# Raw weight tiles moved ahead of all matmul operands, so that weights, x and activations start at one remainder modulo 512 bytes

## The chip, the core and the metric

The kernel runs on one core of a Trainium2 chip. Times are device microseconds (us) of one execution. The kernel before takes 596.16 us (median of 3 runs, 596.13 to 596.34). The execution that was profiled took 596.7 us, and its span from the first to the last instruction is 594.9 us.

A core has TensorE (PE in the profile; its weight loads are listed apart as PEld), VectorE (DVE), ScalarE (ACT), GpSimd (POOL), SyncE (SP, which issues most transfers here) and 16 DMA engines. SBUF is the on-chip memory: 128 partitions, and a tile takes the same stretch of bytes in each of them. PSUM holds the sums that TensorE writes.

## The reference

```
attention (2 batches, 8 heads, 768 positions, 64 wide): a window of 32 positions
    plus one summary key and value per block of 32, softmax  -> x (1536 x 512)
layer 0:  h = x @ w_in;   g = max(0.01 h, h);              x = g @ w_out
layer 1:  h = x @ w_in2;  g = h * tanh(softplus(h));       out = g @ w_out2
w_in 512 x 2048, w_out 2048 x 512; tokens 1536; float32
```

## The kernel before

Attention comes first, interleaved with the first products of layer 0 by an order written out by hand. From about 150 us on there are only the two layers.

**Slots.** The hidden width of 2048 is cut into 16 columns of 128 (f). The 1536 tokens are cut into three blocks j of 512. A slot is one f for one block: "up" (L504) makes h for it, 12 matmuls of 128x128 weights with 512 moving columns; ACT and DVE (and POOL in layer 1) turn h into g; "down" (L559 in layer 0, L566 in layer 1) adds g times the output weights to four sums y, 12 matmuls again. The 12 are four pieces by three products: every operand is held as a high and a low part (float32r), and high*high, high*low and low*high are added. Down lags up by three slots (`LAG = 3`), so TensorE runs up of slot n, down of slot n-3, up of slot n+1, and so on, in groups of 12. L580 is the down step of the last two slots. In up and in down of layer 0 the weights are the operand that is loaded and x or g moves; in down of layer 1, g is loaded and the weights move.

**Parts.** `PARTS = [(0, 6), (0, 10), (1, 10), (1, 6)]`: layer 0 takes its 16 f as 6 and 10, layer 1 as 10 and 6, and each part goes over the three blocks. So the parts have 6, 10, 10 and 6 slots per block.

**Weights.** Each slot's pair of weight tiles has a place k, and a part gives its slots these k, in order: part 0 has 0 to 5; parts 1 and 2 have 6 to 9 and then 0 to 5; part 3 has 6 to 9, 0, 1. A weight block comes by DMA into a `raw` tile (3 buffers, 4104 bytes in a partition, L147), is taken apart by ACT (L158), DVE (L165) and ACT (L194), and its low part is made by POOL or DVE (L201).

**Where tiles stand.** Pools are laid out in the order in which they are opened, each buffer rounded up to 32 bytes, and the pool decides where a tile is:

```
pool = wsp if k < PARTS[0][1] else post
w = pool.tile([P, 2, DM], F32R, tag=f"w{io}_{k}", name="w")
```

`wsp` (places 0 to 5), `xp` (x), `bigp`, `midp`, `l1p` and `gp` (g) follow `const`; then come `rawp` and `padp`. The attention's pools stand behind these, and when the attention is done (`att.close()`), `post` takes the same stretch for the weight places 6 to 9, the temporaries u and r of layer 1 and one more `mid` buffer. Within a weight, x or g tile every operand starts at a multiple of 512 bytes from the tile's start. In the built program of before, `wsp` begins at byte 17280 of a partition, which is 384 modulo 512, and the sizes of all pools up to g are multiples of 512: weights of places 0 to 5 (bytes 21376 on), x (70528 to 119680) and g (148352 on) have remainder 384. The three raw tiles take 4128 bytes each and `two` takes 32, so the attention's pools and later `post` begin at byte 177152, remainder 0.

So 4 of the 10 slots per block in parts 1 and 2, and 4 of the 6 in part 3, use weights at remainder 0 against x and g at 384: 36 slots, 864 matmuls. All other slots have both operands at 384.

Of the kernel before, what the change touches and what calls it, by code (L numbers as in the profile page):

```python
# [9 lines left out]
F32 = mybir.dt.float32  # L10
# [18 lines left out]
def kernel(  # L29
# [18 lines left out]
    P = 128  # L48
# [9 lines left out]
    NS = S // SB  # L58
# [36 lines left out]
    rscale = math.sqrt(D)  # L95

    const = ctx.enter_context(tc.tile_pool(name="const", bufs=1))
    wsp = ctx.enter_context(tc.tile_pool(name="wsp", bufs=1))
    xp = ctx.enter_context(tc.tile_pool(name="xp", bufs=1))
    bigp = ctx.enter_context(tc.tile_pool(name="bigp", bufs=1))  # L100
    midp = ctx.enter_context(tc.tile_pool(name="midp", bufs=4))
    l1p = ctx.enter_context(tc.tile_pool(name="l1p", bufs=2))
    gp = ctx.enter_context(tc.tile_pool(name="gp", bufs=LAG + 1))
    rawp = ctx.enter_context(tc.tile_pool(name="rawp", bufs=3))
    padp = ctx.enter_context(tc.tile_pool(name="padp", bufs=1))
    ps = ctx.enter_context(tc.tile_pool(name="ps", bufs=1, space=PSUM))

    ident = const.tile([P, P], F32, name="ident")
    ind = const.tile([P, 64], F32, name="ind")
    two = padp.tile([P, 1], F32, name="two")  # L110

    nc.scalar.preload_act_table_set("natural_log_exp_and_others")

# [500 lines left out]
    if True:  # L614
# [112 lines left out]
        with tc.manual_schedule(engines={ET.PE, ET.Activation, ET.DVE, ET.Pool}):  # L727
            for word in ORDER.split():
                name, _, banks = word.partition(":")
                eng = engines.get(name[-1])  # L730
                name = name.rstrip("adp") if eng else name
# [100 lines left out]
```

## Time and profile before

| | |
|---|---|
| median of 3 runs | 596.16 us |
| profiled execution | 596.7 us |
| its span | 594.9 us |
| PE busy | 586.1 us, 99% |
| DVE, ACT, POOL busy | 65%, 53%, 33% |

The page gives the busy time of each engine, the granted clock of TensorE, the chain of work that ended last (followed back from the last instruction), and groups of like instructions. Busy time of PE counts a matmul from its start to its modelled end, so consecutive matmuls overlap and a mean of 393 ns says nothing of the pace. The pace is read from the chain: a row "2.72 PE h L504 x12" is 12 matmuls that took 2.72 us of the chain, one after another.

### The profile page before, as it was taken

To read this page: it belongs to the slowest core of one execution; us is meant where nothing else is said; L and a number is where in the kernel's file an instruction comes from. 1 tells how busy PE (TensorE), PEld (TensorE's weight loads), DVE (VectorE), ACT (ScalarE), POOL (GpSimd) and SP (SyncE) were. 2 spreads that over 40 slices of the span, in tenths; PEclk is the share of its full clock that TensorE was granted. 3 is DMA by queue.
4 is the path that set the end of the run, shared out by engine and by line. 5 is a ranking of instruction groups with operands and counts; after the bars stand their busy time and mean duration, and the time that the engine had idled before them with its cause. 6 is when DMAs were issued, how large, how long until landed. Compare 5 with 4: busy or idle time off the path is not lost.

```text
span 594.9 us, 9052 instructions
## 1 busy us (share of the span) xinstructions
PE 586.1 (99%) x3302; PEld 476.0 (80%) x3302; DVE 384.7 (65%) x777; ACT 313.6 (53%) x671; POOL 194.5 (33%) x214
## 2 busy tenths in 40 slices
PE   9799999999999999999999999999999999999997
PEld 4688877787888888888888878888888888888885
DVE  6799865366541123115454998887699988777784
ACT  5878965467741223125655645554476555445442
POOL 6866841184410001003520323232232233232221
PEclk9999999999999999999999999999999999999999
DMA  9996454047631000002536210000022000010011
GB/s 321 331 345 214 161 170 138 2 135 246 221 106 37 0 2 0 1 0 81 171 121 227 74 35 1 0 1 0 1 71 73 0 1 0 2 39 33 0 72 71
DMA packets 19373, 52.10 MB, mean 88 GB/s; under 512 B 2176, under 2 KB 5248, under 8 KB 19072
## 3 DMA queue, kind: packets, MB, share of 16 engines
q1 hardware_dynamic: 18752, 51.00, 26.0%
q8 instruction: 26, 0.43, 0.3%
q10 hardware_dynamic: 576, 0.52, 0.3%
q14 instruction: 19, 0.16, 0.1%
HBM read 48.37 MB, written 3.15 MB: 87 GB/s over the span
## 4 chain that ended last, share of the span: by engine, by line
PE 90%; DMA 5%; ACT 2%; DVE 1%; POOL 0%; issue 0%; SPq 0%; DVEq 0%; ACTq 0%
PE h L504 42%; PE y L566 21%; PE y L559 21%; DMA raw<-in_moe_w_in_dram 3%; PE a L470 2%; PE a L406 2%; PE a L451 1%; DMA v<-in_v_dram 1%; PE y L580 1%; ACT top L158 1%; DMA kT<-in_kT_dram 1%; DVE mid L165 1%; ACT s L430 1%; ACT w L194 0%; ACT g L516 0%; POOL w L201 0%
## 5 line engine op out<-in xcount | busy, mean ns | idle before, releaser
L504 PE MATMUL h<-x,w 128*128 128x512 f32 (+1 forms) x1188 | 287.5, 388 | 0.2 <-ACT g L516 0.2
L504 PEld LDWEIGHTS h<-x,w 128*128 128x128 f32 x1188 | 218.2, 188 | 47.8 <-ACT g L516 0.6
L559 PE MATMUL y<-g,w 128*128 128x512 f32 (+1 forms) x612 | 143.5, 381 | 0.0
L566 PE MATMUL y<-w,g 128*128 128x512 f32 x552 | 136.4, 393 | 0.0
L222 POOL TENSOR_TENSOR g<-e,g 128x512 fp32r<-128x512 f32 x47 | 72.7, 1548 | 185.9 <-ACT g L219 178.3
L559 PEld LDWEIGHTS y<-g,w 128*128 128x128 f32 x612 | 110.1, 189 | 22.4
L566 PEld LDWEIGHTS y<-w,g 128*128 128x128 f32 x552 | 103.5, 188 | 23.8 <-ACT g L219 0.3
L201 POOL TENSOR_TENSOR w<-mid,w 128x512 fp32r<-128x512 f32 x45 | 63.2, 1412 | 106.4 <-ACT w L194 94.8
L520 DVE TENSOR_TENSOR g<-t,g 128x512 fp32r<-128x512 f32 (+1 forms) x51 | 37.2, 731 | 87.5 <-ACT g L516 87.4
L515 ACT ACTIVATE t<-h 128x512 f32<-128x512 f32 (+1 forms) x51 | 28.8, 565 | 90.5 <-PE h L504 90.5
L165 DVE SCALAR_TENSOR_TENSOR mid<-raw,top 128x512 int32<-128x512 int32 x64 | 56.4, 890 | 29.7 <-POOL w L201 17.2
L158 ACT ACTIVATE top<-raw 128x512 f16<-128x512 bf16 x64 | 50.2, 796 | 26.0 <-DMA raw<-in_moe_w_in_dram 10.3
L531 ACT ACTIVATE e<-h 128x512 f32<-128x512 f32 x48 | 28.6, 596 | 61.5 <-PE h L504 54.0
L542 DVE SCALAR_TENSOR_TENSOR u<-u,r 128x512 f32<-128x512 f32 x48 | 36.9, 769 | 25.5 <-ACT r L535 25.1
L534 ACT ACTIVATE r<-u,two 128x512 f32<-128x512 f32 x48 | 34.8, 724 | 30.0 <-DVE u L533 30.0
L430 ACT ACTIVATE s<-s,nm 128x120 f32<-128x120 f32 x96 | 36.6, 385 | 16.7 <-DVE nm L420 16.6
L194 ACT CAST w<-mid 128x512 fp32r<-128x512 f32 x61 | 37.0, 616 | 11.5 <-DVE mid L165 5.9
L219 ACT CAST g<-e 128x512 fp32r<-128x512 f32 x48 | 29.6, 616 | 25.4 <-DVE e L544 25.4
L533 DVE SCALAR_TENSOR_TENSOR u<-e 128x512 f32<-128x512 f32 x48 | 34.6, 721 | 1.1
L445 POOL TENSOR_TENSOR s<-s,r 128x480 f32<-128x480 f32 x24 | 25.0, 1043 | 27.8 <-DVE r L440 15.2
L543 DVE SCALAR_TENSOR_TENSOR u<-u,r 128x512 f32<-128x512 f32 x48 | 33.1, 691 | 1.4
L544 DVE SCALAR_TENSOR_TENSOR e<-e,u 128x512 f32<-128x512 f32 x48 | 33.1, 689 | 1.1
(72 smaller groups left out, 433.3 us busy)
## 6 DMA issues: line engine op xcount, KB each, us to landing
raw<-in_moe_w_in_dram SPq DMA_DIRECT2D x32, 512.0 KB, 3.9
raw<-in_moe_w_out_dram SPq DMA_DIRECT2D x32, 512.0 KB, 3.7
vw<-in_vW_dram SPq DMA_DIRECT2D x24, 192.0 KB, 5.1
kT<-in_kT_dram SPq DMA_DIRECT2D x8, 400.0 KB, 6.6
out_dram<-yp SPq DMA_DIRECT2D x12, 256.0 KB, 2.0
q<-in_qT_dram SPq DMA_DIRECT2D x20, 128.0 KB, 5.2
vS<-in_vS_dram SPq DMA_DIRECT2D x2, 1024.0 KB, 6.8
v<-in_v_dram SPq DMA_DIRECT2D x2, 768.0 KB, 8.9
```

Source lines behind the costliest of these rows:

```text
L158: (tc.keep_in_program_order if pin else id)(nc.scalar.mul(out=do, in_=di, mul=4.0))
L165: nc.vector.scalar_tensor_tensor(out=d, in0=wraw.pop(i)[:, 0:2 * DM].rearrange("p (f w) -> p f w", w=2)[:, :, 1], scalar=13, in1=wtop.pop( ...
L194: nc.scalar.copy(out=w[:, 0], in_=wmid[i])
L201: (eng or nc.gpsimd).tensor_sub(out=w[:, 1], in0=wmid.pop(i), in1=w[:, 0].bitcast(F32))
L222: (nc.vector if lo == "dve" else nc.gpsimd).tensor_sub(out=dst_lo, in0=src, in1=dst_hi.bitcast(F32))
L430: nc.scalar.activation(out=s[:, n], in_=s[:, n], func=AF.Exp, scale=-1.0, bias=nm[:, n:n + 1], accum_out=sm[:, n:n + 1],)
L504: nc.tensor.matmul(ph[:, 0:n], w[:, a, kt * P:(kt + 1) * P], x[:, c, kt, o:o + n], start=(kt == 0 and i == 0), stop=(kt == KT - 1 and i == 2),
L520: (eng or nc.vector).tensor_sub(out=g[:, 1, 0:n], in0=t[:, 0:n], in1=g[:, 0, 0:n].bitcast(F32))
L534: nc.scalar.activation(out=r, in_=u, func=AF.Ln, bias=two[:, 0:1])
L542: V.scalar_tensor_tensor(out=u, in0=u, scalar=2.0, in1=r, op0=ALU.add, op1=ALU.mult)
L559: mm = nc.tensor.matmul(y[d][:, o:o + n], w[:, a, d * P:(d + 1) * P], g[:, c, 0:n], start=sta and not second, stop=sto,)
L566: nc.tensor.matmul(y[d], g[:, a, d * P:(d + 1) * P], w[:, c], start=sta, stop=sto,)
```

## The change

`rawp` is opened directly behind `const`, ahead of `wsp`. The pool `padp` is gone, its tile `two` is in `const`, and `ind` has 44 columns instead of 64 (no slice of it reaches further than column 44).

```
-    wsp = ...   xp ... gp ... rawp ... padp        (order of before)
+    rawp = ctx.enter_context(tc.tile_pool(name="rawp", bufs=3))     (ahead of wsp)
-    rawp = ctx.enter_context(tc.tile_pool(name="rawp", bufs=3))
-    padp = ctx.enter_context(tc.tile_pool(name="padp", bufs=1))
-    ind = const.tile([P, 64], F32, name="ind")
-    two = padp.tile([P, 1], F32, name="two")
+    ind = const.tile([P, 2 * NS - 4], F32, name="ind")
+    two = const.tile([P, 1], F32, name="two")
```

In the built program the instructions of every engine stand in the same order with the same shapes; only addresses differ (and the width of the one memset of `ind`):

| tiles | before: byte, remainder modulo 512 | after |
|---|---|---|
| raw (3) | 164736, 168864, 172992: 384, 416, 448 | 17248, 21376, 25504: 352, 384, 416 |
| weights of places 0 to 5 | 21376 on: 384 | 33728 on: 448 |
| x0, x1, x2 | 86912, 103296, 70528: 384 | 99264, 115648, 82880: 448 |
| g (4) | 148352 on: 384 | 160704 on: 448 |
| attention's q, vw, pT; later weights of places 6 to 9 | 177152 on: 0 | 177088 on: 448 |
| ident | 16512: 128 | 16512: 128 |

## Rows read from the trace of the kernel before

**Rows 1.** Page, part 1: engine, busy us (share of the span), instructions.

```profile
PE 586.1 (99%) x3302; PEld 476.0 (80%) x3302; DVE 384.7 (65%) x777; ACT 313.6 (53%) x671; POOL 194.5 (33%) x214
```

**Rows 2.** Page, part 2: granted TensorE clock in 40 slices, tenths of full.

```profile
PEclk9999999999999999999999999999999999999999
```

**Rows 3.** Page, part 4: the chain that ended last, by engine.

```profile
PE 90%; DMA 5%; ACT 2%; DVE 1%; POOL 0%; issue 0%; SPq 0%; DVEq 0%; ACTq 0%
```

**Rows 4.** Waits of PE, 130 to 595 us: us in total, times, longest.

```profile
PE h L504 <- ACT g L516: 0.2, 1, 0.2
```

**Rows 5.** Chain, 240 to 270 us (part 1): start us, us, what.

```profile
240.06 2.76 PE h L504 x12
242.81 2.79 PE y L559 x12
245.61 2.75 PE h L504 x12
248.36 2.72 PE y L559 x12
...
256.52 2.72 PE h L504 x12
...
261.97 2.79 PE h L504 x12
264.76 2.76 PE y L559 x12
```

**Rows 6.** Chain, 395 to 426 us (part 2, layer 1).

```profile
408.75 2.79 PE y L566 x12
411.54 2.73 PE h L504 x12
414.27 2.72 PE y L566 x12
```

**Rows 7.** Lines of PE, 154.24 to 585.90 us: count | busy us, mean ns | idle.

```profile
L504 PE MATMUL h<-x,w 128*128 128x512 f32 x924 | 227.7, 393 | 0.0
L566 PE MATMUL y<-w,g 128*128 128x512 f32 x552 | 136.4, 393 | 0.0
L559 PE MATMUL y<-g,w 128*128 128x512 f32 x396 | 97.0, 393 | 0.0
```

**Rows 8.** Chain of the whole span: start us, us, what.

```profile
137.50 3.21 DMA raw<-in_moe_w_in_dram
142.56 3.04 PE h L504 x12
...
154.24 2.77 PE y L559 x12
...
348.26 2.89 PE y L566 x12
353.43 2.88 PE y L566 x12
...
585.90 5.47 PE y L580 x24
```

**Rows 9.** Two stretches: us, busy PE, PEld, DVE, ACT, POOL; clock, DMA share, GB/s.

```profile
0.00:50.00 50.00, 44.93 (x574) 35.38 (x574) 41.71 (x166) 38.20 (x136) 36.39 (x81) 1.00 0.99 329
430.00:480.00 50.00, 50.00 (x219) 40.85 (x219) 46.85 (x73) 32.36 (x54) 13.25 (x9) 1.00 0.14 43
```

**Rows 10.** Line L158: duration in ns min/median/max of its 64 instructions.

```profile
L158 ACT ACTIVATE top<-raw x64: 768/796/815, 10.5 to 456.3; 128x512 f16<-128x512 bf16 x64
```

**Rows 11.** Page, part 6: transfers, count, KB each, median us to landing.

```profile
raw<-in_moe_w_in_dram SPq DMA_DIRECT2D x32, 512.0 KB, 3.9
raw<-in_moe_w_out_dram SPq DMA_DIRECT2D x32, 512.0 KB, 3.7
vw<-in_vW_dram SPq DMA_DIRECT2D x24, 192.0 KB, 5.1
q<-in_qT_dram SPq DMA_DIRECT2D x20, 128.0 KB, 5.2
```

More of the change, by code (lines that the diff above doesn't have):

```diff
@@ L97 @@
     const = ctx.enter_context(tc.tile_pool(name="const", bufs=1))
+    rawp = ctx.enter_context(tc.tile_pool(name="rawp", bufs=3))
     wsp = ctx.enter_context(tc.tile_pool(name="wsp", bufs=1))
```

## The prediction

> **What bounds the kernel now.** I read the page first. PE is busy 99% of the span [rows 1], its clock was granted in full in all 40 slices [rows 2], and PE holds 90% of the chain that ended last, DMA 5% [rows 3]. The waits of PE say whether anything else sets its pace behind the attention: from 130 us on they find one wait of 0.2 us [rows 4]. So from about 150 us on the time is the number of matmuls times their pace, and only a change of the pace moves the end.
>
> The pace is in the chain. In part 1, groups of 12 matmuls of the same shape do not take the same time [rows 5]. Up and down groups alternate there, down three slots behind, so each row has its slot. The group at 242.81 is down of the block's fourth slot, whose weights have place 9, remainder 0 against 384 of g: 2.79 us. From 248.36 to 256.52 all operands have remainder 384: 2.72 us each. At 261.97 the next block begins, with place 6 again: 2.79 us. The groups at 245.61 and 264.76 have equal remainders but come right behind a slow group: 2.75 and 2.76 us. Layer 1 shows the same with the operands exchanged, where g is loaded and the weights move: 2.79 us at 408.75, 2.73 behind it, then 2.72 [rows 6]. So there are three paces: 2.72 us (226.7 ns a matmul) where remainders agree, 2.79 to 2.80 (232.5 to 233 ns) where they differ, and something between right behind a slow group.
>
> **The change, part by part.** No instruction is added, removed or moved on any engine or queue; the sum is one of paces.
>
> Weights of places 6 to 9: the 864 matmuls of the 36 slots that use them are 72 groups. At 0.07 to 0.075 us each that is 5.0 to 5.4 us. Equal groups right behind a slow one: in a block of 10 slots the order up, down of three slots earlier gives 7 of them (three downs between the first four ups, then the ups and the down that follow the four slow downs), in a block of 6 slots 4. That is 6 x 7 + 3 x 4 = 54; at 0.01 to 0.04 us (2.73 to 2.76 against 2.72) 0.5 to 2.2 us. Together 5.5 to 7.6 us if every group comes to 2.72.
>
> The whole stretch gives the same sum without a count by hand. From the group at 154.24 to the start of L580 at 585.90 [rows 8] are 431.66 us and 924 + 552 + 396 = 1872 matmuls [rows 7], 156 groups. At 2.72 us they would take 424.3 us: 7.3 us less. Two groups hold a delay that the remainders do not explain, 2.89 and 2.88 us against 2.80 [rows 8]; I leave them their 0.17 us. That makes 7.2 us, the value I take; it is at the upper end of the count by hand, which rounds the groups to 0.01 us.
>
> Ahead of 154 us the weights of places 0 to 5 already agree with x and g, and one slow group falls in front of 142.56, where PE follows a transfer of raw weights (137.50) and the group took 3.04 us [rows 8]. What PE gains ahead of that it waits away: 0. At the end L580 has equal remainders, 5.47 us for two groups, at most 0.03 us more: 0.
>
> The weight transfers of part 2 start when places are freed by PE, so they come earlier with it. The tightest engine behind PE is DVE: 46.85 of 50 us from 430 to 480 [rows 9]. With PE 1.7% faster (7.3 of 431.66) the same work has 49.15 us, 95%. It still fits; if DVE took the lead in that stretch, its 0.85 us of gain would be lost.
>
> Raw tiles move from remainders 384, 416, 448 to 352, 384, 416. L158 reads all three, and its 64 instructions lie between 768 and 815 ns [rows 10]: the start of the tile is worth at most 47 ns of an engine that PE does not wait for. Cost 0; all 64 on the path would be 3 us, which is out, since PE waits for ACT only 0.2 us from 130 us on [rows 4].
>
> Transfers: q and vw now land at remainder 448 instead of 0, in the stretch where DMA is at 0.99 and 329 GB/s [rows 9]. No row shows a price of a start. Raw, which starts off any such border already, has 512 KB landed in 3.7 us where vw at remainder 0 takes 5.1 us for 192 KB [rows 11]; so I take 0. For the other end: two kinds of raw transfers that are alike in size and start differ by 3.9 to 3.7 us, 5% [rows 11], and a price of that size could hide in the rows. vw and q move 24 x 192 + 20 x 128 KB [rows 11], 7.3 MB, 22 us at 329 GB/s; 5% of it, all on the path, is 1.1 us. A gain of the same size has no row for it either, so both ends stay in the range.
> [...]
>
> Sum: the profiled execution was 596.7 us, span 594.9 and 1.8 around it; 594.9 - 7.2 = 587.7, so 589.5 profiled. The median of the runs lies 0.54 lower than the profiled execution: **589.0 us**.
>
> **The rivals.** (a) *No change, 596.2 us.* The slow groups are exactly those that read a tile at byte 177152 or above, and these stay there within 64 bytes. If the place in SBUF is what is slow, and not the remainder, nothing moves. For it: no row has a tile of that place at 384, nor a low tile at another remainder. Against it: the price is the same whether that tile is loaded (2.79 at 242.81) or moves (2.79 at 408.75), and a group that reads no such tile is slowed too when it follows one (2.76 at 264.76) [rows 5, 6], which speaks for how two reads meet. Also, weights, x and g lie up to 140 KB apart and keep 2.72.
> [...]
>
> (b) *Slower, 601 us.* What is fast may be the start 384 and not the agreement: no row has operands at 448. If at 448 every group ran at the slow pace, 156 groups at 2.80 would take 436.8 us instead of 431.66: 5.1 us more. It decides for slower as soon as the mean group is over 2.767 us. For it: only one remainder of agreeing operands is shown. Against it: in every slow group one operand is at 0, and 448 has that no more than 384.
>
> (c) *Less than half the gain, 593.1 us.* The engines behind PE hold it in layer 1, which goes from about 345 to 585.90 [rows 8]: 241 of the 431.66 us, and with them 4.1 of the 7.3 us. If DVE's pace sets the time there, 7.2 - 4.1 = 3.1 us are left. For it: DVE at 94% for 50 us, with 95% to come. Against it: PE's single wait of 0.2 us from 130 us on [rows 4], and three slots between up and down as a reserve.
>
> **How the numbers follow.** Forecast 0.76, (a) 0.10, (b) 0.06, (c) 0.08. A measurement of this kernel tells about 0.2% (1.2 us) from no change. Faster is forecast and (c): 0.84; same is (a): 0.10; slower is (b): 0.06. The forecast's own range is 587.0 to 591.8: the lower end if the delayed groups also come to 2.72 and the transfers gain their 1.1 us (and something is left for rounding), the upper if only the lower count by hand (5.5 us) comes and the transfers lose 1.1 us. Up to 593.5 it takes in (c); what lies outside are (a) and (b), 0.16, and a little of each tail.
>
> **What would show it.** Right: chain groups of 2.72 us throughout parts 1 to 3, with places 6 to 9 not to be told from the others; L580 starting near 578.7; the clock full; everything ahead of 150 us within some tenths. Wrong: rows of 2.79 still there at the first four slots of a block (a); all groups at 2.79 or more (b); waits of PE for ACT, DVE or POOL in layer 1, or a later first up group (c).

## The result, and the profile after

The changed kernel takes 589.88 us (median of 4 runs, 589.78 to 590.40) against 596.14 us before (four runs; the 596.16 above are of three): ratio 0.9888, 95% interval 0.9872 to 0.9903. That is faster by 6.3 us, and 0.9 us over the 589.0 that were forecast. The profiled execution took 589.78 us, its span is 588.0 us.

Lines of the changed kernel are lower by one: L503 is L504 of before, L558 is L559, L565 is L566, L579 is L580. The page's first two parts and the chain by engine read as before [rows 1 to 3]: PE is the bound, with a mean granted clock of 1.000.

```profile
PE 578.0 (98%) x3302; PEld 475.3 (81%) x3302; DVE 384.2 (65%) x777; ACT 313.9 (53%) x671; POOL 193.6 (33%) x214
PEclk9999999999999999999999999999999999999999
PE 90%; DMA 5%; ACT 2%; DVE 1%; issue 0%; POOL 0%; SPq 0%; DVEq 0%; ACTq 0%
```

The chain from 240 to 270 us (start us, us, what) answers to [rows 5]. The group at 241.64 is again down of a block's fourth slot, with weights of place 9, and at 260.68 the next block begins with place 6.

```profile
241.64 2.72 PE y L558 x12
244.36 2.72 PE h L503 x12
247.08 2.72 PE y L558 x12
...
260.68 2.72 PE h L503 x12
263.40 2.72 PE y L558 x12
```

The chain in layer 1, 395 to 426 us, answers to [rows 6]: the slow group of 408.75 is now at 404.87.

```profile
404.87 2.72 PE y L565 x12
407.58 2.72 PE h L503 x12
410.31 2.72 PE y L565 x12
```

Slow groups are gone, and with them the groups slowed behind them. From the chain of the whole span and of 150 to 160 us, to compare with [rows 8]:

```profile
137.90 3.20 DMA raw<-in_moe_w_in_dram
142.95 3.03 PE h L503 x12
...
154.60 2.72 PE y L558 x12
...
578.95 5.45 PE y L579 x24
```

From 154.60 to 578.95 are 424.35 us for the same 1872 matmuls, against 431.66: 7.31 us less. The start of this stretch came 0.36 us later, and behind the start of L579 nothing moved (9.05 against 9.0 us to the span's end). 7.31 - 0.36 - 0.05 = 6.9 us, which is 594.9 - 588.0.

DVE, the engine of rival (c), has 47.44 of 50 us from 430 to 480, 95% (46.85 before [rows 9]), and PE does not wait for it. First the waits of PE from 130 us on, to compare with [rows 4], then the stretch (columns as in rows 9):

```profile
PE h L503 <- ACT g L515: 0.3, 1, 0.3
```

```profile
430.00:480.00 50.00, 50.00 (x223) 41.42 (x222) 47.44 (x74) 31.66 (x53) 12.83 (x9) 1.00 0.13 43
```

### The profile page after: what moved, and what is told of

Its sections match the earlier page's. It is cut to its first block, busy times and chain, and to the rows that moved or that the text cites. A ratio compares the mean times of both kernels' runs of the same rounds, so it can differ in the third digit from the quotient of the medians.

```text
span 588.0 us, 9052 instructions
## 1 busy us (share of the span) xinstructions
PE 578.0 (98%) x3302; PEld 475.3 (81%) x3302; DVE 384.2 (65%) x777; ACT 313.9 (53%) x671; POOL 193.6 (33%) x214
## 4 chain that ended last, share of the span: by engine, by line
PE 90%; DMA 5%; ACT 2%; DVE 1%; issue 0%; POOL 0%; SPq 0%; DVEq 0%; ACTq 0%
PE h L503 42%; PE y L565 21%; PE y L558 21%; DMA raw<-in_moe_w_in_dram 3%; PE a L469 2%; PE a L405 2%; PE a L450 1%; DMA v<-in_v_dram 1%; PE y L579 1%; ACT top L157 1%; DMA kT<-in_kT_dram 1%; DVE mid L164 1%; ACT s L429 1%; ACT w L193 0%; POOL w L200 0%
## 5 line engine op out<-in xcount | busy, mean ns | idle before, releaser
L503 PE MATMUL h<-x,w 128*128 128x512 f32 (+1 forms) x1188 | 283.9, 385 | 0.3 <-ACT g L515 0.3
L503 PEld LDWEIGHTS h<-x,w 128*128 128x128 f32 x1188 | 217.8, 188 | 44.7 <-ACT g L515 0.7
L558 PE MATMUL y<-g,w 128*128 128x512 f32 (+1 forms) x612 | 142.1, 379 | 0.0
L565 PE MATMUL y<-w,g 128*128 128x512 f32 x552 | 134.1, 390 | 0.0
L558 PEld LDWEIGHTS y<-g,w 128*128 128x128 f32 x612 | 110.0, 188 | 21.2
L565 PEld LDWEIGHTS y<-w,g 128*128 128x128 f32 x552 | 103.6, 188 | 21.5 <-POOL g L221 0.2
```

The lines of the kernel that those rows point to most:

```text
L503: nc.tensor.matmul(ph[:, 0:n], w[:, a, kt * P:(kt + 1) * P], x[:, c, kt, o:o + n], start=(kt == 0 and i == 0), stop=(kt == KT - 1 and i == 2),
L558: mm = nc.tensor.matmul(y[d][:, o:o + n], w[:, a, d * P:(d + 1) * P], g[:, c, 0:n], start=sta and not second, stop=sto,)
L565: nc.tensor.matmul(y[d], g[:, a, d * P:(d + 1) * P], w[:, c], start=sta, stop=sto,)
```

## The experiments

The theory after the result: a group is slow when the two operands that TensorE reads from SBUF, the one that it loads and the one that moves, start at different remainders. The trace of before could not part this from rival (a), the place of the post pool, nor from a rival (d), that remainder 0 itself is slow. Nor did any row show which differences cost, and whether 512 is the right modulus. All kernels below compute the whole reference. "Place n" is the place k of a weight tile; a difference is given modulo 256 where that is said. Chains are as above: start us, us, what. Ratios are to the kernel before, measured beside each experiment.

**Agreement at the old place (e1).** The kernel before, with nothing but a gap ahead of `post`:

```
         att.close()
+        gapp = ctx.enter_context(tc.tile_pool(name="gapp", bufs=1))
+        gapp.tile([P, 96], F32, name="gap")
         post = ctx.enter_context(tc.tile_pool(name="post", bufs=1))
```

> The kernel before, with a gap of 384 bytes between the attention's place and the post pool and nothing else: weights of places 6 to 9 go from remainder 0 to 384 and so agree with x and g, while raw, the attention's tiles and all other weights keep their addresses. Agreement of remainders (my theory): all groups 2.72 us, first group behind 145.59 us where it was in the kernel before, total near 589.4 us (596.1 less 6.9, no later start). Place in SBUF is slow (rival a): no change, 596.1 us. Remainder 0 is slow whatever it meets (rival d): also 589.4, so the next run has to tell this one from the theory.

Measured: 589.72 us against 596.89 in the same session, ratio 0.9881 (0.9866 to 0.9896). Its chain, at the block's end and start:

```profile
143.07 3.02 PE h L504 x12
...
241.75 2.72 PE y L559 x12
244.47 2.72 PE h L504 x12
...
260.79 2.72 PE h L504 x12
```

Rival (a) falls: the tiles moved by 384 bytes, stayed at the end of SBUF, and their groups take 2.72 us. The change's whole gain is there with raw left where it was; what helps is only the remainder of `post`. The first row is a miss of the expectation: it comes at 143.07, not at the 142.56 of before [rows 8], although raw, q, vw and the weights of places 0 to 5 have the addresses of before. The difference is there early: the first raw transfer of the chain ends at 21.06 us in before, at 21.41 in e1 and at 21.39 in the changed kernel (in this order; its start and its length add up to that).

```profile
12.64 8.42 DMA raw<-in_moe_w_in_dram
12.47 8.94 DMA raw<-in_moe_w_in_dram
12.56 8.83 DMA raw<-in_moe_w_in_dram
```

**All at remainder 0 (e2).** The changed kernel with 64 bytes more in `const`:

```
     two = const.tile([P, 1], F32, name="two")
+    const.tile([P, 16], F32, name="gap")
```

> The changed kernel with a gap of 64 bytes at the end of const: raw at remainders 416, 448, 480, everything from the weights on at remainder 0, which agree with each other, and q and vw land at 0 as in the kernel before. Agreement: all groups 2.72 us. Rival d (0 itself is slow): groups at 2.80 us, 600 us or more. If the 0.4 us by which the changed kernel reached its first steady group later (145.99 against 145.59) comes from q and vw at 448, it is gone here and the total is 589.4; if it comes from the raw tiles' starts or from chance, it may stay, 589.9.

Measured: 589.36 us, ratio 0.9879 (0.9862 to 0.9895).

```profile
142.38 3.03 PE h L504 x12
...
241.06 2.72 PE y L559 x12
243.78 2.72 PE h L504 x12
```

Rival (d) falls in its plain form: 0 against 0 is fast. The row at 142.38 together with e1's at 143.07 says more on the start: with q and vw at remainder 0 in both, it lies 0.7 us apart (raw starts elsewhere in e2), and before and e1, with raw, q and vw at the same addresses, are 0.5 us apart. So the 0.4 us by which the changed kernel was later is within what executions differ by there, and no price of landing at 448 is shown. A price of some tenths is not excluded either: with q and vw at 448, the changed kernel and e3 to e8 have this row at 142.82 or later, and the three profiles with 0 have it at 142.38, 142.56 and 143.07.

**Differences of 64 and 256 (e3, e4).** The changed kernel with the gap of e1 ahead of `post`, 64 and 256 bytes:

```
+        gapp.tile([P, 16], F32, name="gap")      (e3; 64 columns in e4)
```

> The changed kernel with a gap of 64 bytes ahead of the post pool: weights of places 6 to 9 at remainder 0 against 448, a difference of 64 instead of the 128 of the kernel before. If any disagreement costs the same: 2.80 us for the 72 groups, 596.5 us. If the price grows with the distance: between, near 593 us. If only a difference of 128 or more counts: 589.9 us.

> The changed kernel with a gap of 256 bytes ahead of the post pool: weights of places 6 to 9 at remainder 192 against 448, a difference of 256, half of 512; neither operand is at 0. Any disagreement costs the same: 2.80 us for the 72 groups, 596.5 us. Price grows with distance: above 2.80, 600 us or more. What matters is modulo 256 and not 512, or only remainder 0 is slow: 589.9 us.

Measured: e3 596.82 us, ratio 1.0002 (0.9990 to 1.0013), the whole gain lost; e4 589.91 us, ratio 0.9888 (0.9873 to 0.9902), nothing lost. First e3 in part 1 and in layer 1, then e4 at the block's start in part 1:

```profile
237.72 2.80 PE y L558 x12
240.52 2.75 PE h L503 x12
...
408.90 2.76 PE y L565 x12
411.67 2.77 PE h L503 x12
...
422.60 2.72 PE h L503 x12
```

```profile
206.13 2.72 PE h L503 x12
208.85 2.72 PE y L558 x12
211.57 2.72 PE h L503 x12
```

A difference of 64 costs the whole gain, and one of 256, half of 512, costs nothing. So what has to agree is the remainder modulo 256. In layer 1 of e3 the slow group is 2.76, not 2.80; there the weights move and g is loaded, so the difference has the other sign. The group behind it, whose operands agree, takes 2.77, no less than the one that disagrees.

**Differences of 128, 32 and 192 (e5, e6, e8).** The same gap with 128, 32 and 192 bytes.

> The changed kernel with a gap of 128 bytes ahead of the post pool: weights of places 6 to 9 at remainder 64 against 448, a difference of 128 as in the kernel before, but with neither operand at 0. Agreement modulo 256 (theory, after the run with 256 cost nothing): 2.80 us for the 72 groups, total as before, 596.5 us. Rival d' (a slow group needs one operand at 0 and the other not): 2.72 us, 589.7 us.

> The changed kernel with a gap of 32 bytes ahead of the post pool: remainder 480 against 448. If every difference modulo 256 costs in full: 596.5 us. If a step of 64 bytes is what counts: 589.7 us. If the price grows within a step: between.

> The changed kernel with a gap of 192 bytes ahead of the post pool: remainder 128 against 448, which modulo 256 is the difference of 64 in the other direction. If the direction doesn't matter: 2.80 us, 596.5 us as with 64. If only differences one way cost: 2.72 us, 589.7 us.

Measured: e5 597.15 us, ratio 1.0010 (1.0000 to 1.0019); e6 596.81 us, ratio 1.0007 (0.9998 to 1.0017); e8 593.95 us, ratio 0.9955 (0.9940 to 0.9970). The chains at the start of a block in part 1, for e5, e6 and e8, and then those of e8 and e6 in layer 1:

```profile
208.72 2.80 PE h L503 x12
211.51 2.76 PE y L558 x12
```

```profile
207.15 2.79 PE h L503 x12
209.95 2.73 PE y L558 x12
```

```profile
206.58 2.75 PE h L503 x12
209.33 2.72 PE y L558 x12
```

```profile
401.33 2.80 PE y L565 x12
404.13 2.74 PE h L503 x12
```

```profile
403.02 2.80 PE y L565 x12
405.83 2.76 PE h L503 x12
```

In e5 no operand is at 0 and it is as slow as before, so (d) falls in every form. In e6, 32 bytes cost in full: the border below which a difference is free, if there is one, lies under 32. In layer 1 of e6 the difference is 224, and it costs in full too (2.80). e8 fits neither of its two expectations. Its up groups cost 2.75 and its layer 1 2.80; e3 was the mirror image, 2.80 and 2.76. Both are one rule if the difference is taken as loaded less moving, modulo 256: 64 costs 0.08 us a group (part 1 in e3, layer 1 in e8), 192 costs 0.03 to 0.04 (layer 1 in e3, up in e8). With 32 and 224 the direction makes no such difference. What follows a slow group differs as well: behind 192 in part 1 of e8 the next group takes 2.72 and is not slowed at all, behind 32 in part 1 of e6 it takes 2.73, behind 128 in e5 2.76.

**High and low half apart (e7).** The changed kernel with 128 bytes between the halves of the tiles of places 6 to 9:

```
-        w = pool.tile([P, 2, DM], F32R, tag=f"w{io}_{k}", name="w")
+        if pool is wsp:
+            t = pool.tile([P, 2, DM], F32R, tag=f"w{io}_{k}", name="w")
+            w = (t[:, 0], t[:, 1])
+        else:
+            t = pool.tile([P, 2 * DM + 32], F32R, tag=f"w{io}_{k}", name="w")
+            w = (t[:, 0:DM], t[:, DM + 32:])
```

> The changed kernel with 128 bytes between the high and the low half of the weight tiles of places 6 to 9 alone. Their up tiles then have the high half agreeing with x and the low half off by 128; their down tiles the other way round. An up group's matmuls go (high w, high x), (high w, low x), (low w, high x). If a matmul is slow when it disagrees with its own loaded weights, starts are 233 ns apart behind the third of each three; if it is slow when the weights loaded during it disagree (those of the next matmul), behind the second of each three. Either way 432 of the 864 matmuls are slow, so about half of the loss: near 593 us. If the price were one for a whole tile by its start, ups would be fast and downs slow, also near 593 us, but with all matmuls of an up group at 226.7 ns.

Measured: 594.69 us, ratio 0.9968 (0.9955 to 0.9980): not near 593, about 4.8 of the 6.8 us between the changed kernel (589.88) and before (596.65, measured beside e7) are lost, and not half. The chain has up groups of places 6 to 9 at 2.77 us and the down groups of places 0 to 5 between them at 2.72:

```profile
212.51 2.77 PE h L508 x12
215.28 2.72 PE y L563 x12
218.00 2.77 PE h L508 x12
```

From the starts of the matmuls in those up groups, from 150 us on: behind the first of three 227.0 ns to the next start (mean of 142), behind the second 232.3 (143), behind the third 234.0 (143). The price is not one of a whole tile. But the second (whose own weights agree, and whose successor's don't) and the third (the other way round) are both slow, so my question of own or next weights stays open: one disagreeing load in three costs about 13 ns, spread over two starts, where a matmul in a group that disagrees throughout costs about 6. Nor does the price add up load by load: the down groups of places 6 to 9, in which two matmuls of three disagree, take 2.81 us in part 1, no less than a whole group that disagrees, and 2.75 in layer 1.

```profile
237.36 2.81 PE y L563 x12
...
402.16 2.75 PE y L570 x12
```

**Roles exchanged (e9).** The changed kernel with `ind` between l1p and gp:

```
+    indp = ctx.enter_context(tc.tile_pool(name="indp", bufs=1))
     gp = ctx.enter_context(tc.tile_pool(name="gp", bufs=LAG + 1))
-    ind = const.tile([P, 2 * NS - 4], F32, name="ind")
+    ind = indp.tile([P, 2 * NS - 4], F32, name="ind")
```

> The changed kernel with ind taken out of const and laid between l1p and gp: weights of places 0 to 5 and x are at remainder 0 modulo 256, g and the weights of places 6 to 9 at 192. So the roles are exchanged: in layer 0 the down groups of places 0 to 5 now disagree (loaded less moving: 64) and those of places 6 to 9 agree; the up groups of places 6 to 9 disagree by 192 and those of 0 to 5 agree. By loaded less moving modulo 256 (theory, prices per group from the runs before: 64 about 0.08 us, 192 about 0.03 in up and 0.05 in down of layer 1): down of layer 0 with low weights 2.80 us, down of places 6 to 9 2.72 to 2.76, and in all 36 x 0.03 + 36 x 0.08 + 24 x 0.05 = 5.2 us and up to 3 for groups behind slow ones: 595 to 598 us. By the place of the tile: down groups of places 0 to 5 stay at 2.72 us and those of places 6 to 9 are the slow ones.

Measured: 596.90 us, ratio 1.0001 (0.9992 to 1.0011). The chain over a block's end and start in part 1; at 238.70 and 244.19 the down groups have places 6 to 9, from 249.69 on places 0 to 5:

```profile
238.70 2.73 PE y L559 x12
241.43 2.76 PE h L504 x12
244.19 2.73 PE y L559 x12
...
249.69 2.80 PE y L559 x12
...
255.23 2.80 PE y L559 x12
258.02 2.74 PE h L504 x12
...
263.57 2.79 PE h L504 x12
...
269.16 2.76 PE h L504 x12
```

The weights that never were slow are slow now, and those of `post` agree with g and take 2.73 us. The rule carries over to tiles that the change did not make agree.

Two things in these rows go beyond it. The up group at 241.43 (weights of place 2 and x, both at 0) agrees, and so do the down groups before and behind it (both operands at 192); it takes 2.76 us all the same. So a group that agrees can be slowed without a slow group ahead of it, where the remainder changes from one group to the next. And up groups of places 6 to 9, with a difference of 192, take 2.76 to 2.79 here behind a down group with 64 (263.57 and 269.16), so 0.03 is not all that 192 can cost.

The starts of the matmuls show what such groups have in common. Behind PE's one wait in the changed kernel, where every operand agrees, the group at 142.95 (3.03 us, shown above) has nine intervals of 225 to 237 ns, 231 in the mean, before it is back at 226 to 227. The up groups of e9 that follow an agreeing group of another remainder have intervals of the same kind (224 to 236 ns, for about ten matmuls). So what was called the pace right behind a slow group looks like a settling of the pace after a disturbance, be it a wait or a change of remainder; why it lasts so long is not shown.

No experiment gave a version that is clearly faster than the changed kernel: e1, e2 and e4 have intervals that overlap with its.

## Why the prediction was right, and where it was off

**The bound.** Right: the time is matmuls times pace from 150 us on, before and after; PE's waits from 130 us on are 0.3 us against 0.2.

**The three paces.** Right for this kernel: 2.72, 2.79 to 2.80 and the one behind a slow group were read from rows of before, and removing the disagreement brought every group of the steady stretch to 2.72, but for one at 2.75 (350.44 us) of which the next paragraph speaks. What the third pace hangs on was read too simply: e8 has none behind groups of 2.75 in part 1, and e9 has it where no slow group stands ahead. The sum from the whole stretch gave 424.3 us for 156 groups; 424.35 were measured. The count by hand (5.5 to 7.6 us) holds that too, at its upper end.

**The two delayed groups.** Off by a little: I left them their 0.17 us, but one is gone in the changed kernel and the other is 0.03 us late, as the stretch of 424.35 us against 156 x 2.72 = 424.3 shows. The steady gain is 7.31 us, not 7.2. It is not agreement that freed them. In the trace of before a load (PEld) waits 0.3 us for g in each of the two; in the changed kernel one such wait of 0.2 us is left; e1, where everything agrees as well, has both groups late (2.85 and 2.89 us), and e2 and e4 have none.

**Start of the steady part.** I set it at 0 with 1.1 us either way. It came 0.36 us later, nearly all of it from the first raw transfer (0.33 us); e1, with the addresses of before, has as much, and e1 and e2 show a scatter of 0.7 us at the later row, so it is not to be put down to where q and vw land. My reason for 0 was weak: raw's 3.7 us against vw's 5.1 [rows 11] compares transfers under different load, as the DMA share is 0.99 in the first 50 us and 0.14 from 430 to 480 [rows 9]. I also left out four transfers of q that the queue of ACT issues, 0.5 MB.

**The median.** The profiled execution of before lay 0.54 us over its median and I carried that over; the one of after lay 0.1 under its own. That and the later start are the term that was mis-sized: 0.36 + 0.64 - 0.1 (steady part) = 0.9 us, the distance of 589.0 from 589.88.

**The rivals.** (a) was refuted by e1 and e9: places 6 to 9 are fast in the old place when they agree, and places 0 to 5 are slow when they don't. (b) did not happen: agreement at 384, 448 and 0 gives the same 2.72 us. (c) did not happen: DVE at 95% did not hold PE.

**What the prediction left too narrow.** It spoke of remainders modulo 512. The runs show 256, and for one pair a direction: differences of 32, 64, 128 and 224 (loaded less moving) cost in full, 192 about a third to a half. No other difference was run. Nothing in the time forecast hung on this, since the change makes the difference 0.

The same matmuls took 2.79 to 2.80 us a group before and 2.72 in e1, where nothing but the place of one of their two operands differs. So the pace of a group hangs on the addresses of both operands together; waits of PE for other engines, 0.2 us in all from 130 us on before [rows 4] and 0.3 in the changed kernel, are not what makes the difference.

## What to carry to other kernels

Where TensorE is the bound and its pace differs between groups of the same shape, compare the start addresses of the loaded and the moving operand: here they should be equal modulo 256 (2.72 us a group against 2.79 to 2.80 at differences of 32, 64, 128 and 224, 2.75 to 2.79 at 192), and a pool of odd size in front of some of the operands is enough to spoil it. One remainder for all of them is better than agreement pair by pair: in e9 groups that agree took 2.73 to 2.76 us where the remainder changed between groups. The smallest remedy was a gap ahead of the one pool that was off (e1); moving the odd pool to the front does the same. Read the pace from the chain's groups, not from the mean duration, which was 393 ns in the steady stretch before and 390 after.

## What the runs showed of the hardware

- Float32r matmuls of 512 columns with a 128x128 load for each follow one another every 226.7 ns at a granted clock of 1.000 when loaded and moving operands agree modulo 256 bytes, and every 232.5 to 233 ns in the mean when loaded less moving is 32, 64, 128 or 224.
- A difference of 192 gives 2.75 to 2.76 us a group where 64 gives 2.80; behind a group with 64 it was up to 2.79 (e9).
- A group that agrees takes 2.72 to 2.77 us behind one that does not: 2.72 behind 192 in part 1 of e8, 2.77 behind it in layer 1 of e3. It takes 2.73 to 2.76 behind one that agrees at another remainder (e9), and after a plain wait of 0.3 us the starts are as uneven, 225 to 237 ns apart, for nine matmuls (changed kernel, 142.95 us). Why this lasts, and why the price of one disagreeing load goes over two starts (e7: 232.3 and 234.0 ns), was not settled.
